# Routing in two parts: three experts' first tiles ahead of the last batch, and the loads of v on another queue

## The chip, the cores and the metric

The kernel runs on one core of one Trainium2 chip. The metric is device microseconds (us) from launch to end. Three runs of the kernel before took 190.79, 191.17 and 836.14 us; the median is 191.17. The program runs its engines from queues of instructions, one for each engine, in the order in which the program lists them: TensorE (PE in the profile), VectorE (DVE), ScalarE (ACT), GpSimd (POOL) and SyncE (SP). SyncE, ScalarE and GpSimd also issue transfers (DMAs), which run on 16 shared transfer engines.

## The reference

```python
scores = q @ k^T / 8                      # 4 batches, 8 heads, 768 positions, 64 per head, float32
# heads 0, 2, 6: causal; the others: causal and (first 4 positions or the last 64)
attn = softmax(masked scores) @ v
x = attn as 3072 tokens of 512            # token = (batch, position)
do_compute = x @ w_skip > 0
e = argmax(x @ w_gate) ; g = max softmax  # 8 experts
out = x ;  out[do_compute] += g * relu(x @ w1[e]) @ w2[e]      # w1 512 x 1024, w2 1024 x 512, float32
```

## The kernel before, in words

**Two plans.** All work is given to a small planner, class `Plan` (L53). `op(name, eng, dur, fn, deps, key)` lists one step with the engine, an assumed duration, what it needs and a key; `dma(...)` (L71) lists a step that issues a transfer and a second one on a queue "Q", which stands for the transfer engines. `lay` (L77) goes through time: whenever an engine is free, the ready step with the smallest key starts. What comes out is only an order: `write` calls the steps' functions in the order of their planned starts, and each engine's queue holds its instructions in that order. On the chip each instruction waits for what it needs, and everything behind it on its engine waits with it. The first plan holds attention and routing, the second the experts.

**Attention.** 16 pairs of heads, numbered `i`, four to a batch. For a pair, SyncE loads q and k (`load_pair`, L644, issue at L650, 384 KB each, in pieces of 6 x 64 floats) into 12 shared buffers, so a load waits for the cast (`Cq`, `Ck`, L702) six pairs before. v comes for a whole batch (`load_v`, L654, issue at L661, pieces of 64 floats): batch 0's in two parts, batches 1 to 3 in one, all on SyncE, into two buffers `vf`. GpSimd casts q, k and v to float16 (L702, `Cv` L708) and lays out parts of k and v for the windowed heads (`Kx` L777, `Vx` L813). TensorE transposes (L730, L741), computes scores (`E`, L876 and L888), ScalarE takes the exp (`X`, L898), TensorE weighs v (`PV`, L940), which also carries the products of v with `w_gate` and `w_skip` as 9 more columns (L795). VectorE divides (`Nr`, `Nl`, `Nx`, L959 to L976); after each batch SyncE stores x to `out` (`xo`, L985; the last batch in three parts) and VectorE sums the batch's logits (`Gs`, L991).

**Weights.** `w1` and `w2` of 8 experts are 16 tiles of 1 MB in float16 (`w1_0` is tile 0, `w2_0` tile 1, ...). GpSimd issues them (L439), cast on the way, mostly in halves of 512 KB. Six tiles have room of their own during attention; `PARTS` says after which step each half may be issued, and in which order:

```python
PARTS = [("Vx", i) for i in (9, 9, 10, 10, 13, 14, 14, 15)]
PARTS += [("r", 0, "R", 12), ("r", 0, "L", 15), ("r", 0, "L", 15)]
```

The other tiles take room that attention leaves, in the second plan.

**Routing** (`route`, L1051). Each token that computes gets a slot: expert `e` has 256 slots, two tiles of 128, `t = 2e` and `2e + 1`. Tokens are 24 columns of 128; columns 0 to 17 are the first three batches, 18 to 23 the last. Phase 0 handles 18 columns, phase 1 the last 6: maximum, expert, one-hot (L1106 to L1115), on TensorE the ranks within the expert (L1088 to L1095), two tables (L1156, L1164 and L1172), and on TensorE the product of the tables, which puts token number and gate into the slots (`slots`, L1193). In the kernel before, both phases add up in one product and one index, `idx` and `gsl` (L1246 to L1250): no tile is known until phase 1 is done. Phase 0's tables are made on GpSimd, phase 1's on VectorE.

**Experts.** For each tile ScalarE writes zeros (`z`, L1281), GpSimd gathers the rows of `out` by `idx` (L1286), VectorE casts (`cx`, L1313), TensorE transposes (`tx`, L1322), VectorE copies (`ox`, L1333). For an expert, first product on both tiles at once (`F`, L1344, 256 columns), ReLU on ScalarE (`Re`, L1354), second product for each tile (`Y`, L1365), VectorE scales and adds (`A`, L1371), GpSimd scatters the rows back (`S`, L1299). One list, `gorder`, fixes the order of gathers and of the remaining halves of weights on GpSimd (a half, two gathers, a half, ...), with at most eight of them on their way. The last tile, 15, comes in a half and two quarters.

## Time and profile before

| what | us |
|---|---|
| median of three runs | 191.17 |
| the profiled execution, its own time | 192.18 |
| its span, first to last instruction | 190.5 |
| busy: PE, DVE, ACT, POOL | 148.3, 108.6, 102.3, 133.0 |
| `idx` written (start of L1248) | 107.88 |
| first gather, first product of an expert | 108.95, 115.33 |
| last weights waited for | 180.32 |

The page divides the span into 40 slices of 4.76 us; each digit is a busy share in tenths, and 9 is 90% or more. The DMA row is the mean share of the 16 transfer engines. In a table by stage, each line has the stretch, its length, busy time and count for PE, PEld (weight load of TensorE), DVE, ACT and POOL, then the clock that TensorE was granted, the share of the transfer engines, and GB/s. Packets of two queues can overlap on one engine, so a share can be a little over 1. A line of the timeline has the start, the length, the engine, the line of the kernel, the operation and its operands; what stands in brackets is the idle time before it and what ended it. "SPq" is SyncE's queue: an issue that lasts long stands at the head of the queue and holds what is behind it.

### The profile page before, as it was taken

How to read it: one execution, taken by the hardware profiler on the slowest of the kernel's cores; microseconds unless marked ns; L12 is line 12 of the kernel's file. 1: busy time of each engine (PE TensorE's matmuls, PEld its weight loads, DVE VectorE, ACT ScalarE, POOL GpSimd, SP SyncE). 2: the span in 40 equal slices, each digit the busy share in tenths (PEclk: the TensorE clock that was granted, in tenths of full speed). 3: DMA queues.
4: the chain of work that ended last, by engine and by line, in shares of the span. 5: the costliest groups of instructions: out<-in, count | busy, mean ns of one | idle time of the engine just before them, and what ended most of it. 6: DMA issues, size and time to landing. Idle time of an engine off the chain costs nothing.

```text
span 190.5 us, 4641 instructions
## 1 busy us (share of the span) xinstructions
PE 148.3 (78%) x1832; PEld 117.2 (62%) x1832; DVE 108.6 (57%) x234; ACT 102.3 (54%) x137; POOL 133.0 (70%) x233
## 2 busy tenths in 40 slices
PE   0688988399999999999922118799999999999700
PEld 0567776388988888878722007768687695638300
DVE  6576457436788769798999524356556434032020
ACT  2595977268899898999769700440340430402100
POOL 7575985969999999987599188788885234354540
PEclk9999999889999999999996555999999999999975
DMA  5999959997899699999999978999999999999720
GB/s 169 332 342 317 313 159 357 385 363 249 242 373 376 193 333 268 213 284 284 213 247 272 206 131 221 227 261 246 223 229 212 191 242 214 243 236 245 189 91 3
DMA packets 29184, 47.12 MB, mean 247 GB/s; under 512 B 5204, under 2 KB 21460, under 8 KB 29154
## 3 DMA queue, kind: packets, MB, share of 16 engines
q0 software_dynamic: 7312, 21.55, 53.1%
q1 hardware_dynamic: 20512, 24.78, 39.4%
q10 hardware_dynamic: 1330, 0.41, 0.9%
q8 instruction: 16, 0.26, 0.6%
q14 instruction: 14, 0.11, 0.2%
HBM read 56.64 MB, written 10.49 MB: 352 GB/s over the span
## 4 chain that ended last, share of the span: by engine, by line
DMA 33%; PE 25%; SPq 11%; DVE 10%; POOL 9%; issue 7%; ACT 2%; POOLq 0%; ACTq 0%
DMA w<-in_moe_w_dram 18%; SPq L650 10%; PE pst L888 8%; DMA out_dram<-xg,idx 6%; PE pst L876 6%; PE opsa L940 4%; POOL xg L1286 3%; DMA kf<-in_k_dram 3%; PE tps L730 3%; DMA xg<-out_dram,idx 3%; POOL out_dram L1299 3%; DMA qf<-in_q_dram 2%; PE tps L741 2%; DVE k L770 2%; ACT k L768 1%
## 5 line engine op out<-in xcount | busy, mean ns | idle before, releaser
L898 ACT ACTIVATE at<-pst 128x1024 f16<-128x1024 f32 (+1 forms) x60 | 58.8, 1013 | 12.8 <-PE pst L888 12.4
L1354 ACT ACTIVATE ht<-hps 128x512 f16<-128x512 f32 x32 | 16.7, 602 | 52.2 <-PE hps L1344 46.4
L888 PE MATMUL pst<-qT,k 128*128 128x128 f16 (+2 forms) x308 | 36.0, 236 | 0.1
L1344 PE MATMUL hps<-xT,w 128*128 128x256 f16 x256 | 31.6, 281 | 1.7 <-DMA w<-in_moe_w_dram 1.1
L770 DVE COPY k<-tps 64x768 f16<-64x768 f16 x27 | 25.8, 954 | 11.7 <-PE tps L730 10.3
L1344 PEld LDWEIGHTS <-w 128*128 128x128 f16 x256 | 29.1, 145 | 4.6 <-DMA w<-in_moe_w_dram 2.4
L1365 PE MATMUL yps<-w,ht 128*128 128x512 f16 x128 | 29.6, 379 | 1.3 <-ACTq L1470 1.1
L888 PEld LDWEIGHTS <-k 128*128 128x128 f16 x308 | 24.6, 99 | 9.3 <-issue 2.6
L1299 POOL DMA_INDIRECT out_dram<-xg,idx x16 | 16.6, 1040 | 17.6 <-DMA out_dram<-xg,idx 6.2
L1371 DVE SCALAR_TENSOR_TENSOR xg<-yps,gsl,xg 128x512 f32<-128x512 f32 x16 | 11.8, 749 | 21.5 <-PE yps L1365 20.9
L439 POOL DMA_DIRECT2D w<-in_moe_w_dram x33 | 19.0, 579 | 6.5 <-DMA w<-in_moe_w_dram 6.3
L1286 POOL DMA_INDIRECT xg<-out_dram,idx x16 | 17.3, 1084 | 8.8 <-DVE gsl L1250 4.2
L876 PE MATMUL pst<-smask,identb 128*128 128x512 bf16 (+2 forms) x64 | 22.0, 353 | 1.6 <-ACT at L898 1.6
L940 PE MATMUL opsa<-va,at 128*128 128x74 f16 x392 | 20.7, 199 | 0.6 <-DVE x L976 0.6
L1365 PEld LDWEIGHTS <-ht 128*128 128x128 f16 x128 | 12.2, 98 | 14.7 <-ACTq L1470 1.3
L940 PEld LDWEIGHTS <-at 128*128 128x128 f16 x472 | 19.0, 99 | 0.8 <-DVE x L976 0.8
L1313 DVE CAST x<-xg 128x512 f16<-128x512 f32 x16 | 9.5, 624 | 12.3 <-DMA xg<-out_dram,idx 10.6
L708 POOL CAST va<-vf 128x768 f16<-128x768 f32 x16 | 13.2, 825 | 2.7 <-PE opsa L940 1.6
L976 DVE TENSOR_TENSOR x<-opsa,recs 128x768 f32<-128x768 f32 x15 | 14.2, 943 | 0.0
L702 POOL CAST k<-kf 128x768 f16<-128x768 f32 x15 | 12.3, 822 | 2.3 <-DMA kf<-in_k_dram 1.9
L756 ACT COPY qT<-tps 128x768 f16<-128x768 f16 x16 | 12.8, 798 | 1.9 <-PE tps L730 1.7
L702 POOL CAST q<-qf 128x768 f16<-128x768 f32 x14 | 11.5, 822 | 3.0 <-DMA qf<-in_q_dram 2.3
(131 smaller groups left out, 227.5 us busy)
## 6 DMA issues: line engine op xcount, KB each, us to landing
w<-in_moe_w_dram POOLq DMA_DIRECT2D x31, 512.0 KB
qf<-in_q_dram SPq DMA_DIRECT2D x16, 384.0 KB, 7.4
kf<-in_k_dram SPq DMA_DIRECT2D x15, 384.0 KB, 6.6
out_dram<-x SPq DMA_DIRECT2D x3, 1536.0 KB, 12.5
out_dram<-x SPq DMA_DIRECT2D x1, 768.0 KB, 13.2
out_dram<-x SPq DMA_DIRECT2D x2, 384.0 KB, 10.9
w<-in_moe_w_dram POOLq DMA_DIRECT2D x2, 256.0 KB
kf<-in_k_dram ACTq DMA_DIRECT2D x1, 384.0 KB, 4.4
```

What stands on the lines that cost most here:

```text
L439: nc.gpsimd.dma_start(out=wts[e, half][:, c], in_=(w1r, w2r)[half][e][:, c])
L650: eng.dma_start(out=t.rearrange("p (h n) d -> p h (n d)", n=NQB), in_=rows6[w][i // 4, :, h0:h0 + 2])
L702: e.tensor_copy(t, f)
L770: nc.vector.tensor_copy(to, ti)
L876: nc.tensor.matmul(pst[:, c0 - c * CH:c0 - c * CH + m].rearrange("p (n c) -> p n c", c=P), identb, mv, start=(n == 0), stop=(n == last))
L888: nc.tensor.matmul(pst[:, c0 - c * CH:c0 - c * CH + m * P], lt, qTs[i][:, qb * P:(qb + m) * P], start=(n == 0), stop=(n == last))
L898: nc.scalar.activation(ats[i][:, c * CH:c * CH + cn], psts[i, c][:, :cn], ACT.Exp, scale=SCALE)
L940: nc.tensor.matmul(opss[i][:, hi, qb * VA:(qb + 1) * VA], ats[i][:, b0 + c:b0 + c + P], vb, start=(n == 0), stop=(n == len(todo) - 1))
L1286: h = nc.gpsimd.indirect_dma_start(out=xgs[:, t], out_offset=None, in_=out[:, :], in_offset=bass.IndirectOffsetOnAxis(ap=idx[:, t:t + 1], ...
L1299: h = nc.gpsimd.indirect_dma_start(out=out[:, :], out_offset=bass.IndirectOffsetOnAxis(ap=idx[:, t:t + 1], axis=0), in_=xgs[:, t], in_offs ...
L1344: nc.tensor.matmul(hpss[e, f2][:, fi, :], w1[:, s, 2 * f2 + fi], xTs[e][:, s, :], start=(fi == 0 and s == 0), stop=(fi == 1 and s == DS - 1))
L1365: nc.tensor.matmul(ypss[t], hts[e][:, j, s2 * P:(s2 + 1) * P], w2[:, j], start=(j == 0), stop=(j == FS - 1))
```

## The change

1. `load_v` issues batches 1, 2 and 3 on ScalarE's queue, each after a given exp (pairs 0, 4, 8); batch 0 stays on SyncE. 
2. Phase 0 gets an index of its own (`idxA`). The first tile of each expert is filled from the first three batches alone: `full` is the expert's count over them, but at least 128, and phase 1's ranks begin there, so that the last batch's tokens go into the second tile. Where three batches give fewer than 128, the rest of the first tile stays empty. Second tiles are completed by phase 1, whose tables now have 8 columns in place of 16.
3. The first tiles of experts 0, 1 and 2 (`KA = 3`) are gathered after `idxA`, in buffers that attention leaves, and go through cast, transposes, both products, ReLU and add in the first plan, beside phase 1. The second plan has 13 tiles left; first tiles of experts 3 to 7 may also be gathered before `idx`. The scatters of the early tiles come after `idx`.
4. `PARTS` has 12 halves in place of 11, ten of them tied to pairs 8 to 14. `gorder` has a new order. Batch 2's x is stored in two parts.
5. The planner's transfers take turns between queues, several durations are changed, and most keys (`K`) have new values, which may change the order on every engine.

```diff
-    PARTS = [("Vx", i) for i in (9, 9, 10, 10, 13, 14, 14, 15)]
-    PARTS += [("r", 0, "R", 12), ("r", 0, "L", 15), ("r", 0, "L", 15)]
+    PARTS = [("Vx", i) for i in (8, 8, 8, 9, 10, 12, 12, 13, 13, 14)]
+    PARTS += [(("G", 0), "go"), (("G", 4), "go")]
...
-                nc.sync.dma_start(out=vs32[b][:, h0 * NQB:h1 * NQB],
-                                  in_=rows1["v"][b, :, h0 * NQB:h1 * NQB])
+                eng = nc.scalar if b else nc.sync
+                eng.dma_start(out=vs32[b][:, h0 * NQB:h1 * NQB],
+                              in_=rows1["v"][b, :, h0 * NQB:h1 * NQB])
...
+        VAT = (0, 1, 5, 9)
...
-                dma(("ld",) + o, "SP", 0.45, 196.6 * (h1 - h0), load_v(b, h0, h1),
-                    [("Cv", 4 * b - 5)], next(sp),
-                    rate=228 if h1 - h0 == 2 else 305)
+                dma(("ld",) + o, "ACT" if b else "SP", 0.6, 196.6 * (h1 - h0),
+                    load_v(b, h0, h1),
+                    [("Cv", 4 * b - 5), VAT[b] and ("X", VAT[b] - 1, 0)],
+                    -99 if b else next(sp), rate=228 if h1 - h0 == 2 else 300, turn=0.22)
...
-        for b in range(B - 1):
+        for b in range(B - 2):
             dma(("xo", b), "SP", 0.5, 1573, x_out(b, 0, DM),
-                [("Nx", 4 * b + 3)], next(sp) - 2.5 * (b < 2))
+                [("Nx", 4 * b + 3)], next(sp) - 2.5)
+        dma(("xo", 2, 9), "SP", 0.5, 787, x_out(2, 0, 256), [("Nx", 9)], next(sp))
+        dma(("xo", 2), "SP", 0.5, 787, x_out(2, 256, DM), [("Nx", 11)], next(sp))
...
                 if ph:
                     nc.tensor.matmul(
                         rk, ones16,
-                        cnt[:, 0:1, :E].to_broadcast([P, n, E]),
+                        full.unsqueeze(1).to_broadcast([P, n, E]),
                         start=False, stop=True)
+                else:
+                    nc.tensor.matmul(r[:, n * E:(n + 1) * E], ones16,
+                                     cnt[:, 0, :E], start=False, stop=True)
...
+            def rsel_full():
+                v.tensor_mul(rsel, rk(), o)
+                if ph == 0:
+                    v.tensor_scalar(full, T[ph, "rk"][:, n * E:(n + 1) * E],
+                                    float(P), 1.0 / P, ALU.max, ALU.mult)
+                    v.tensor_copy(cnt[:, 0, :E], full)
...
+        def fin_a():
+            m = sm_pool.tile([P, NT, 4], FP32, name="msb")
+            v = nc.vector
+            v.tensor_copy(m, T["mps", 0])
+            for n, (i, g) in enumerate(((idx[:, ::2], gsl[:, ::2]),
+                                        (idx0, gsl0))):
+                v.scalar_tensor_tensor(i, m[:, n::2, 1], float(P), m[:, n::2, 0],
+                                       ALU.mult, ALU.add)
+                v.tensor_tensor(g, m[:, n::2, 2], m[:, n::2, 3], op=ALU.add)
+
+        op("idxA", "DVE", 0.8, fin_a, [("r", 0, "slots")], K["sl"])
...
+        for j in range(0, 2 * KA, 2):
+            op(("zA", j), "ACT", 0.95, zero_a(j), [("Cv", 15)], 146 + j)
+        for a in range(KA):
+            t = 2 * a
+            dma(("G", t), "POOL", 1.05, 150, gather(t),
+                [("zA", t), "idxA", ("xo", 2), ("xo", 2, 9), ("G", t - 2, "go")], 152)
+            op(("cx", t), "DVE", 0.6, cast_a(t), [("G", t), ("tx", t - 4)],
+               165 + a)
+            op(("tx", t), "PE", 0.25, turn_a(t), [("cx", t)], 165 + a,
+               take=("tps", ("ox", t)))
+            op(("ox", t), "DVE", 0.42, out_a(t), [("tx", t), ("Fa", t - 4, 1)],
+               165 + a)
+            for h in range(2):
+                op(("Fa", t, h), "PE", 0.92, first_a(t, h),
+                   [("ox", t), ("W", t, 0), ("W", t, 4), ("X", *seq[-2]),
+                    ("X", *seq[-1]), ("Re", t - 4, 1)], 168 + a)
+                op(("Re", t, h), "ACT", 0.6, relu_a(t, h),
+                   [("Fa", t, h), ("PV", 15, 1), ("Ya", t - 4)], 168 + a)
+            op(("Ya", t), "PE", 1.75, second_a(t),
+               [("Re", t, 0), ("Re", t, 1), ("W", t + 1, 0), ("W", t + 1, 4),
+                ("Nx", 15), ("Nl", 15)]
+               + ([("A", t - 4), ("A", t - 2)] if a % 2 == 0 else []), 168 + a)
+            op(("A", t), "DVE", 0.75, add(t), [("Ya", t)], 168 + a)
...
-        gorder = [("g", 0), ("g", 1)]
-        gets, late = list(range(2, NT)), late
-        while gets:
-            gorder.append(late.pop(0))
-            gorder += [("g", t) for t in gets[:2]]
-            gets = gets[2:]
+        gorder, gets = [], [6, 8, -1, 1, -1, 3, 5, -1, 10, 7, -1, 12, 9, -1, 14, 11,
+                            -1, 13, -1, 15]
+        for t in [-1] + gets:
+            gorder.append(("g", t) if t >= 0 else late.pop(0))
         gorder += late
...
+        for a in range(KA):
+            dma(("S", 2 * a), "POOL", 1.0, 150, scatter(2 * a), ["idxB"], 2 * a)
```

In the diff, `("G", t)` is a gather, its `"go"` the issue; `-1` in `gets` is the next half of weights; `zero_a`, `cast_a`, `turn_a`, `out_a`, `first_a`, `relu_a` and `second_a` do for one tile what the experts' steps above do, the first product on 128 columns.

More of the change, by code (lines that the diff above doesn't have):

```diff
@@ L39 @@
 NT = E * CAP // P
+KA = 3
+N0 = 3 * S
 NPR = B * H // 2
@@ L53 @@
 class Plan:
-    LAT = dict(PE=0.26, DVE=0.1, ACT=0.12, POOL=0.12, SP=0.1, Q=1.9)
+    LAT = dict(PE=0.26, DVE=0.1, ACT=0.12, POOL=0.12, SP=0.1, Q=2.1)
     def __init__(self):
@@ L714 @@
         CASTER["q", 0], CASTER["k", 0], CASTER["q", 1] = "DVE", "ACT", "DVE"
-        took = dict(POOL=0.85, DVE=0.6, ACT=0.85)
+        took = dict(POOL=0.83, DVE=0.6, ACT=0.85)
         for i in range(NPR):
@@ new lines, with zero_a, go, row @@
+        op("idx", "DVE", 0.7, fin, [("r", 1, "slots")], 200)
+        xga = {}
+        def zero_a(j):
+            def go():
+                if j == 0:
+                    xga[0] = v_pool.tile([P, 2 * KA, DM], FP32, tag="v",
+                                         name="xga")
+                nc.scalar.copy(
+                    xga[0][:, j:j + 2],
+                    zero1.unsqueeze(2).to_broadcast([P, 2, DM]))
+            return go
+        def row(t):
+            return xga[0][:, t] if t < 2 * KA else xgs[:, t - 2 * KA]
@@ new lines, in moved, with gather, go @@
+        def moved(h):
+            tc.declare_no_dep(
+                h.ins, group="rows",
+                reason="each token is in one slot, so slots share no row")
+            tc.add_to_no_dep_group("rows", h.ins)
+        def gather(t):
+            def go():
+                n = N if t % 2 else N0
+                moved(nc.gpsimd.indirect_dma_start(
+                    out=row(t), out_offset=None, in_=out[:n, :],
+                    in_offset=bass.IndirectOffsetOnAxis(
+                        ap=idx[:, t:t + 1], axis=0),
+                    bounds_check=n - 1, oob_is_err=False))
+            return go
@@ new lines, in scatter, with go, add @@
+        def scatter(t):
+            def go():
+                n = N if t % 2 else N0
+                moved(nc.gpsimd.indirect_dma_start(
+                    out=out[:n, :], out_offset=bass.IndirectOffsetOnAxis(
+                        ap=idx[:, t:t + 1], axis=0),
+                    in_=row(t), in_offset=None,
+                    bounds_check=n - 1, oob_is_err=False))
+            return go
+        def add(t):
+            return lambda: nc.vector.scalar_tensor_tensor(
+                row(t), ypss[t], gsl[:, t:t + 1], row(t), ALU.mult, ALU.add)
```

310 lines of the change are left out of this document (192 added, 118 removed).

## The prediction

> **What bounds the kernel now.** I read the page first (the slices, the chain, the queues), then a table by stage, then the transfer issues of SyncE, and last the routing and the tail in the timeline.
>
> ```profile
> DMA  5999959997899699999999978999999999999720
> DMA 33%; PE 25%; SPq 11%; DVE 10%; POOL 9%; issue 7%; ACT 2%; POOLq 0%; ACTq 0%
> ```
> The 16 transfer engines stand at 9 nearly everywhere, and transfers and SyncE's issues together lead the chain. So I cut the table by stage at the places where that row dips (the last two columns are the transfer engines' share and GB/s):
> ```profile
> 0.00:3.00 3.00, 0.00 (x0) 0.00 (x0) 1.70 (x5) 0.00 (x0) 2.17 (x11) 1.00 0.22 53
> 3.00:23.00 20.00, 15.04 (x199) 12.07 (x200) 13.04 (x36) 14.86 (x17) 13.84 (x26) 1.00 1.07 336
> 23.00:29.00 6.00, 5.40 (x98) 4.56 (x94) 3.31 (x7) 4.70 (x6) 5.20 (x11) 1.00 0.62 171
> 29.00:44.00 15.00, 11.29 (x171) 9.72 (x172) 7.59 (x14) 8.84 (x11) 10.89 (x20) 0.89 1.06 364
> 44.00:48.00 4.00, 3.81 (x62) 3.15 (x60) 2.87 (x6) 3.49 (x5) 3.65 (x9) 1.00 0.70 226
> 48.00:53.00 5.00, 5.00 (x93) 4.42 (x91) 4.37 (x8) 4.51 (x6) 4.77 (x12) 1.00 0.90 259
> 53.00:63.00 10.00, 10.00 (x181) 8.77 (x179) 8.39 (x16) 9.34 (x11) 9.16 (x25) 1.00 1.06 375
> 63.00:67.00 4.00, 3.60 (x63) 3.02 (x60) 2.71 (x7) 3.32 (x5) 3.76 (x9) 1.00 0.55 153
> 67.00:110.00 43.00, 30.90 (x540) 26.44 (x538) 35.52 (x82) 36.57 (x51) 34.00 (x64) 0.90 1.06 258
> 110.00:118.00 8.00, 3.80 (x21) 2.94 (x22) 2.29 (x5) 0.00 (x0) 6.47 (x8) 0.50 0.79 175
> 118.00:178.00 60.00, 56.35 (x419) 41.03 (x418) 25.36 (x52) 16.67 (x32) 35.29 (x44) 1.00 1.05 230
> 178.00:190.50 12.50, 3.09 (x14) 1.07 (x12) 1.41 (x2) 0.00 (x0) 3.83 (x4) 0.71 0.23 72
> ```
> Full stages show a share of 1.05 to 1.07. From 3 to 178 us the engines are full but for five holes: 23-29 (6 x 0.38 = 2.28 us), 44-48 (4 x 0.30 = 1.20), 48-53 (5 x 0.10 = 0.50), 63-67 (4 x 0.45 = 1.80) and 110-118 (8 x 0.21 = 1.68), **7.46 us** in all. That the share is a real limit, and not a queue that is merely never empty, shows in a stretch that holds weights alone and in one that holds them with the scatters:
> ```profile
> 74.00:82.00 8.00, 8.00 (x137) 6.85 (x136) 6.67 (x14) 7.17 (x9) 7.58 (x15) 1.00 1.05 205
> 126.00:160.00 34.00, 33.80 (x254) 24.31 (x252) 17.55 (x39) 9.47 (x19) 20.99 (x26) 1.00 1.05 224
> w<-in_moe_w_dram POOLq DMA_DIRECT2D x31, 512.0 KB
> ```
> A half of a weight tile, 512 KB as it lands, takes 0.524/0.205 = 2.56 us by the first row, 32 halves 82 us. After 126 us the rate hardly moves. TensorE is full there too, but it isn't what ends last: at the end it waits for weights.
> ```profile
> 180.32 1.02 PE L1365 MATMUL yps<-w,ht 128*128 128x512 f16 x4 [0.26 <-DMA w<-in_moe_w_dram]
> 180.95 1.41 DVE L1371 SCALAR_TENSOR_TENSOR xg<-yps,gsl,xg 128x512 f32<-128x512 f32 x2 [5.70 <-PE yps L1365]
> ```
> The last weights land at 180.3; from there 10.2 us of product, add, scatter and close remain, and the change leaves that tail alone. So I forecast when the transfers are done: what the transfers weigh, plus their holes.
>
> **Where the holes are from.** The issues of SyncE (start, length):
> ```profile
> 13.63 0.71 SPq L661 DMA_DIRECT2D vf<-in_v_dram  x1
> 14.39 10.14 SPq L650 DMA_DIRECT2D qf<-in_q_dram  x1
> 34.31 0.71 SPq L661 DMA_DIRECT2D vf<-in_v_dram  x1
> 35.17 8.92 SPq L650 DMA_DIRECT2D qf<-in_q_dram  x1
> 51.09 0.71 SPq L661 DMA_DIRECT2D vf<-in_v_dram  x1
> 51.89 13.77 SPq L650 DMA_DIRECT2D qf<-in_q_dram  x1
> ```
> Each load of v for a batch is issued in 0.71 us, and then the next load of q stands in the queue for 8.9 to 13.8 us: until 24.5, 44.1 and 65.7. The three larger early holes lie at exactly these ends. So SyncE is let go only when the engines have nearly run dry, and they stay thin until new loads flow. Four holes, 5.78 us, I put down to this.
>
> **The change part by part.**
>
> *v of batches 1 to 3 on ScalarE's queue.* Nothing stands behind v on SyncE then, and q and k of later pairs are issued while v moves. Gain: between 0 (the hole goes elsewhere) and 5.78 us. I take three quarters, **4.3 us**, nearer the upper end because the stalls and the holes coincide three times out of three; not all, because a pair's load still waits for the cast six pairs before it, and once these buffers are full the engines may thin out again. The hole at 63-67 is covered twice: ten halves of weights are now tied to the pairs up to 14, from pair 8 on, where eight were tied to 9 to 15. The cost on ScalarE is three issues at 0.71 us by the rows above. Queued behind each is an exp, which the weighing on TensorE awaits; 2.1 us at most if nothing covered them. Attention has room to pay:
> ```profile
> 20.00:38.00 18.00, 13.46 (x212) 11.40 (x211) 10.42 (x17) 12.38 (x15) 14.70 (x29) 0.96 0.91 300
> 38.00:95.00 57.00, 55.93 (x950) 48.15 (x948) 44.05 (x91) 50.05 (x56) 48.83 (x110) 0.98 0.98 283
> ```
> TensorE idles 4.5 us from 20 to 38, where the first stall of SyncE over 10 us is felt, and 1.1 us in the 57 after it. With q and k ahead of v, attention ends some 3 us earlier, which by itself is worth nothing at the end: it brings the buffers free sooner. I count the three issues at 0.
>
> *The split routing.* The tables of the first three batches are made on GpSimd after the last pair as before; what is new is a slot product and five small VectorE operations, then three gathers.
> ```profile
> 98.90 4.76 POOL L1164 TENSOR_TENSOR tables<-r_ohi,r_olo 128x384 f16<-128x384 f16 x6
> 103.24 1.15 PE L1193 MATMUL mps<-tables 128*128 128x64 f16 x18
> 107.88 0.19 DVE L1248 SCALAR_TENSOR_TENSOR idx<-msb 128x16 int32<-128x16 f32 x1
> 108.95 1.09 POOL L1286 DMA_INDIRECT xg<-out_dram,idx  x1 [4.21 <-DVE gsl L1250]
> 113.68 1.13 PE L1322 MATMUL xtp<-ident,x 128*128 128x128 f16 x8 [6.09 <-DVE x L1313]
> ```
> The tables end at 103.7. Product and index take 1.15 + 5 x 0.19 = 2.1 us, less the 3 us that attention may gain: first early gather near 103 to 106 in place of 108.95, first early transposes 4.7 us behind it (108.95 to 113.68), near 108 to 111. SyncE's part is one more issue for batch 2's x, early enough to be landed. GpSimd's queue to idx is now: gather, half a tile, two gathers, two halves, two gathers (experts 3 and 4), a half, and then the gather that waits for idx. These four halves are 4 x 2.56 = 10.2 us of transfers, and cover the hole at 110-118. I take **1.2 us** of its 1.68 (bounds 0 and 1.68), since some descriptors are still written while the engines wait.
> What the wait holds up: behind that gather stand all later weights on GpSimd. VectorE's own path to idx loses two operations of 0.2 us, and may have the casts, copies and adds of three tiles ahead of it:
> ```profile
> L1371 DVE SCALAR_TENSOR_TENSOR xg<-yps,gsl,xg 128x512 f32<-128x512 f32 x16 | 11.8, 749 | 21.5 <-PE yps L1365 20.9
> L1313 DVE CAST x<-xg 128x512 f16<-128x512 f32 x16 | 9.5, 624 | 12.3 <-DMA xg<-out_dram,idx 10.6
> L1333 DVE COPY xT<-xtp 128x512 f16<-128x512 f16 x16 | 6.6, 423 | 10.6 <-PE xtp L1322 10.3
> ```
> 3 x (0.75 + 0.62 + 0.42) = 5.4 us: idx comes between 0.4 us earlier and 5.4 us later, from about 105. Their keys (165 to 168) stand behind the routing's (150), so I take 1 us. The 10.2 us of halves cover all of it; without them it would cost up to 5.4.
>
> *Three tiles multiplied early.* An expert takes 7.39 us of TensorE from one first product to the next:
> ```profile
> 137.93 3.66 PE L1344 MATMUL hps<-xT,w 128*128 128x256 f16 x32
> 145.32 1.47 PE L1344 MATMUL hps<-xT,w 128*128 128x256 f16 x12
> ```
> Half of it for each of three tiles, 11.1 us, moves ahead of idx. 13 tiles are left, 13/16 x 8 x 7.39 = 48 us; even from 120 they end at 168, ahead of the last weights. So this part frees TensorE and moves the end by **0**: weights arrive at 2 x 2 x 2.56 = 10.2 us an expert, and 7.39 us of work hides under that. The zeros on ScalarE, the 16 gathers and the 16 scatters keep their number.
>
> **Sum.** 4.3 + 0 + 1.2 + 0 = 5.5 us off the span of 190.5: 185.0. The profiled execution itself took 192.18 us, so 186.7; the median of the runs is 191.17, so **185.7**.
>
> **Rivals.**
>
> *All holes close, and the end thins out less.* 7.46 us, and about 1.5 us more of the last stretch before 180.3, where TensorE, now ahead, no longer delays scatters: 191.17 - 9.0 = 182.2. For it: v on its own queue and earlier weights cover most holes twice. Against: loads still wait for buffers.
>
> *The queue is not the cause.* Transfers from either queue end on the same 16 engines; if the thinning belongs to v's own end, moving its issue saves only the 0.71 us of issuing, the holes move with v, and 1.2 us is left: 190.0. For it: the engines were over 1.0 while SyncE stood, so nothing was lost then. Against: the next q is issued only when the hole is there.
> The Trainium skill has this as a rule (DMA: Bandwidth & Descriptors, "Issuing engines are not separate DMA queues"): starting transfers from several engines saves only the time to issue them; by that rule this rival is the outcome, and the trace bears it out as far as share and rate go, not for what stands behind v.
>
> *Slower: v starves beside q and k.* Two queues now share the engines. By the loads in the code a piece of q or k is 6 x 64 x 4 = 1,536 bytes and one of v 64 x 4 = 256, and the page has packets of both kinds:
> ```profile
> DMA packets 29184, 47.12 MB, mean 247 GB/s; under 512 B 5204, under 2 KB 21460, under 8 KB 29154
> 24.20 0.82 POOL L708 CAST va<-vf 128x768 f16<-128x768 f32 x1
> ```
> If the queues alternate piece by piece, v has 256/1,792 = 14% of the 336 GB/s; if they share evenly, half. 1.57 MB then takes 33 or 9 us from about 11: batch 1's v lands between 20 and 44. Its first cast stood at 24.2 in GpSimd's queue, with later casts of q and k behind it, for which TensorE waits. It decides once v lands after 33.8: 24.2, the 4.5 us that TensorE now idles, and 2 x 2.56 us of the two halves more that are tied to pairs and keep the engines full. At 39, halfway from there to the end, attention is 5 us late, with batch 2 as late again 10 us, and half of the gains remain: 191.17 + 10 - 2.7 = 198.5. No row shows loads of both kinds from two queues side by side, so I can't exclude it.
> The Trainium skill (DMA: Bandwidth & Descriptors, "Queues, rings and completion order") says that each engine takes turns between its queues by whole packets of several descriptors; by that rule, with several pieces to a packet, v's part is nearer the 14%, and no run here shows it yet.
>
> **How the numbers follow.** Forecast 0.53 (own range 183.5 to 188.0), all holes 0.13, queue not the cause 0.23, slower 0.11. A measurement of this kernel tells about 2% from no change: the bounds are 187.35 and 195.0. Faster: 0.50 of the forecast and 0.13, 0.63; within: 0.03 and 0.23, 0.26; slower 0.11. The range, 182.0 to 191.0, leaves out half of the second case and the slow one, 0.17.
>
> **What would show it.** Right: no issue of q over 5 us behind v; shares near 1.05 from 23 to 67 and from 110 to 118; first products on TensorE before 112, and TensorE waiting for weights from 130 on; the last weights near 175 with 10 us behind them. Wrong: holes of the same size after v has moved; a v cast waiting for its transfer; a gap in the weights while GpSimd waits for idx.

## The result, and the profile after

The changed kernel takes 208.37 us (median of 4 runs, 207.52 to 210.04) against 190.98 for the kernel before beside it: a ratio of 1.0951 with a 95% interval of 1.0835 to 1.1067. It is 17.4 us slower; I had forecast 5.5 us faster. Its profiled execution took 209.07 us, with a span of 207.4. Executions of one kernel scatter (its profiled one and its median can lie 2 to 4 us apart, and one run of the kernel before and one of e8 below took 836 us), so profiles below say where time lies, and medians and ratios how much it is; for two experiments the scatter leaves no ratio.

The row of the transfer engines and the chain on the page of the changed kernel:
```profile
DMA  6999949999949918999999950599999999999310
PE 32%; DMA 25%; issue 14%; POOL 12%; DVE 8%; ACT 6%; ACTq 0%; POOLq 0%
```
Transfers no longer lead the chain. Where the row had shallow dips it now has a 5, a 0 and a 5 in slices 24 to 26, and a 1 in slice 15, counted from 1. The table by stage of the changed kernel, with the cuts of the prediction and some new ones (columns as there; the last two are the transfer engines' share and GB/s):
```profile
23.00:29.00 6.00, 5.24 (x89) 4.34 (x87) 4.71 (x8) 4.35 (x5) 4.21 (x10) 1.00 0.57 170
44.00:48.00 4.00, 4.00 (x62) 3.55 (x61) 1.87 (x4) 3.14 (x5) 1.99 (x6) 0.72 1.05 369
53.00:63.00 10.00, 9.88 (x171) 8.67 (x170) 8.74 (x17) 9.25 (x11) 7.63 (x15) 1.00 0.75 262
63.00:67.00 4.00, 3.93 (x71) 3.45 (x69) 2.95 (x7) 3.38 (x5) 3.53 (x14) 1.00 1.12 347
67.00:80.00 13.00, 10.56 (x176) 8.83 (x174) 7.61 (x15) 10.00 (x12) 12.46 (x25) 1.00 0.64 165
110.00:118.00 8.00, 1.41 (x15) 1.16 (x16) 4.35 (x18) 0.00 (x0) 4.91 (x5) 0.57 1.02 292
118.00:134.00 16.00, 12.98 (x126) 9.77 (x123) 3.71 (x7) 8.07 (x11) 3.64 (x4) 0.90 0.37 73
```
The holes at 44-48, 63-67 and 110-118 are closed, as forecast (though with attention later, as shown below, these times hold other work than before). The one at 23-29 is as it was (0.57, before 0.62). New ones stand at 53-63 (10 x 0.31 = 3.1 us against a full share of 1.06), 67-80 (13 x 0.42 = 5.5) and, above all, 118-134 (16 x 0.69 = **11.0**). In sum 19.6 us of new holes; gone are those at 44-48, 48-53, 63-67 and 110-118 (1.4 + 0.8 + 2.0 + 2.2 = 6.4 by the same measure, less 0.3 left at 110-118). That leaves 13.5 of the 16.9 us between the two spans.

What happens at 118-134, from the timeline and the waits of GpSimd, ScalarE and TensorE in the changed kernel:
```profile
109.13 0.17 DVE L1300 SCALAR_TENSOR_TENSOR idx<-msb 128x8 int32<-128x8 f32 x1
110.19 1.12 POOL L1342 DMA_INDIRECT xga<-out_dram,idx  x1 [2.22 <-DVE r_gate L1164]
114.53 1.18 POOL L460 DMA_DIRECT2D w<-in_moe_w_dram  x2
116.69 0.17 DVE L1312 TENSOR_TENSOR idx<-msc 128x8 int32<-128x8 f32 x1
124.25 3.11 PE L1397 MATMUL hpa<-xTa,w 128*128 128x128 f16 x48
128.43 4.82 ACT L1475 COPY xg<-zero 128x1024 f32<-128x1024 f32 x5
129.75 1.06 POOL L1342 DMA_INDIRECT xg<-out_dram,idx  x1 [14.04 <-ACT xg L1475]
132.15 0.60 POOL L460 DMA_DIRECT2D w<-in_moe_w_dram  x1
```
The three early gathers go out, two halves of weights follow at 114.5, and then GpSimd stands for 14.0 us before the gather of tile 6, the first of the second plan. It waits for ScalarE to write its zeros, and these start only when the last early first product has ended (124.25 + 3.11 = 127.4). The half of weights behind it leaves at 132.15. So from 120 to 132 there is little to move. The index is not what it waits for: tile 6 needs only `idxA` (109.13), and even the full index was there at 116.7.

The reason lies in the storage. The rows of the second plan, `xg`, are 10 tiles in a pool (`moe_xg`) that is opened after the pool of the weights (`moe_w`), and so lies over attention's buffers for q and k in float16. The early tiles keep their cast and transposed rows (`x16a`, `xTa`) in these very buffers (pool `qk`, tags `q16` and `k16`). The zeros may not be written until TensorE has read them for the last time.

Attention ends later too, by 105.72 - 98.23 = 7.5 us, where I had it some 3 us earlier. The last pair's division, in the kernel before and in the changed one:
```profile
98.23 0.22 DVE L959 RECIPROCAL recs<-opsa 128x12 f32<-128x12 f32 x1
```
```profile
105.72 0.23 DVE L987 RECIPROCAL recs<-opsa 128x12 f32<-128x12 f32 x1 [1.34 <-PE opsa L968]
```

### The profile page after: what moved, and what is told of

The parts are those of the page before. It is cut to its first block, busy times and chain, and to the rows that moved or that the text cites. A ratio compares the mean times of both kernels' runs of the same rounds, so it can differ in the third digit from the quotient of the medians.

```text
span 207.4 us, 4844 instructions
## 1 busy us (share of the span) xinstructions
PE 154.8 (75%) x1929; PEld 123.3 (59%) x1929; DVE 108.1 (52%) x241; ACT 102.2 (49%) x140; POOL 132.8 (64%) x233
## 4 chain that ended last, share of the span: by engine, by line
PE 32%; DMA 25%; issue 14%; POOL 12%; DVE 8%; ACT 6%; ACTq 0%; POOLq 0%
PE pst L916 8%; DMA out_dram<-xg,idx 7%; DMA w<-in_moe_w_dram 6%; PE hps L1520 6%; DMA xga<-out_dram,idx 5%; PE opsa L968 5%; DMA qf<-in_q_dram 4%; PE pst L904 4%; PE tps L758 4%; ACT at L926 3%; POOL out_dram L1352 3%; PE yps L1543 2%; DVE k L798 2%; DMA kf<-in_k_dram 2%; POOL q L730 2%
## 5 line engine op out<-in xcount | busy, mean ns | idle before, releaser
L1531 ACT ACTIVATE ht<-hps 128x512 f16<-128x512 f32 x26 | 13.7, 602 | 46.0 <-PE hps L1520 34.2
L1520 PE MATMUL hps<-xT,w 128*128 128x256 f16 (+1 forms) x256 | 28.0, 273 | 3.8 <-DMA w<-in_moe_w_dram 3.8
L1520 PEld LDWEIGHTS <-w 128*128 128x128 f16 x256 | 25.9, 148 | 6.5 <-DMA w<-in_moe_w_dram 5.0
L1543 PE MATMUL yps<-w,ht 128*128 128x512 f16 x104 | 24.2, 382 | 0.0
L1342 POOL DMA_INDIRECT xg<-out_dram,idx x10 | 10.7, 1067 | 16.8 <-ACT xg L1475 14.0
L1360 DVE SCALAR_TENSOR_TENSOR xg<-yps,gsl,xg 128x512 f32<-128x512 f32 x10 | 7.4, 750 | 22.7 <-PE yps L1543 22.3
L1352 POOL DMA_INDIRECT out_dram<-xg,idx x10 | 10.0, 1002 | 13.4 <-DVE xg L1360 7.1
L1543 PEld LDWEIGHTS <-ht 128*128 128x128 f16 x104 | 10.1, 99 | 10.9 <-issue 0.7
L805 POOL COPY kx<-k 64x256 f16<-64x256 f16 x20 | 8.2, 412 | 10.6 <-DVE k L798 6.0
L758 PE MATMUL tps<-ident,k 128*128 128x128 f16 x96 | 8.3, 224 | 6.2 <-ACT k L727 6.2
L784 ACT COPY qT<-tps 128x768 f16<-128x768 f16 x16 | 12.8, 800 | 0.1
```

The source lines that it names most:

```text
L758: nc.tensor.matmul(t[:, n], c16[w, i][:, n].rearrange("p h d -> p (h d)"), C.ident, is_transpose=True, start=(n == 0), stop=(n == NQB - 1))
L1352: moved(nc.gpsimd.indirect_dma_start(out=out[:n, :], out_offset=bass.IndirectOffsetOnAxis(ap=idx[:, t:t + 1], axis=0), in_=row(t), in_offs ...
L1520: nc.tensor.matmul(hpss[e, b][:, fi, :], w1[:, s, m * b + fi], xTs[e][:, s, :w], start=(fi == 0 and s == 0), stop=(fi == m - 1 and s == DS ...
L1543: nc.tensor.matmul(ypss[t], hts[e][:, j, n * P:(n + 1) * P], w2[:, j], start=(j == 0), stop=(j == FS - 1))
```

## The experiments

Theory after the first look: the changed kernel loses most by the room that `xg` shares with the early tiles, and the rest by a later attention. Rivals: the order on ScalarE or the split itself is at fault; v on ScalarE's queue does gain, as forecast, and only the rest costs. All ratios are against the kernel before on the same chip.

### Is it the room? (e1, e2)

```diff
-    with tc.tile_pool(name="moe_w", ...) as mw_pool, \
-         tc.tile_pool(name="moe_xg", ...) as xg_pool, \
+    with tc.tile_pool(name="moe_xg", ...) as xg_pool, \
+         tc.tile_pool(name="moe_w", ...) as mw_pool, \
```


> Changed kernel, with the buffer for the second plan's 10 tiles allocated ahead of the weight tiles, so that it lies over the buffers of the loads of q and k (read for the last time during attention) and no longer over the buffers that the early tiles' cast and transposed rows use. Theory 'storage': gather 6 waited 14 us on GpSimd for early tiles to be done with that room, and all weights stood behind it; the thin stretch of the transfer engines from 120 to 134 (10.4 us) goes, and the time falls from 208.4 to about 198. Rival 'the early tiles themselves are too slow or too late': the transfers stay thin there for another reason, 205 to 208.

Measured: 197.58 us, ratio 1.0448 [1.0373, 1.0523]. Two lines changed places and 10.8 us are gone between the medians, 5.0 points (hundredths) of the ratio. The stretch in this kernel:
```profile
118.00:134.00 16.00, 14.20 (x147) 10.95 (x145) 6.48 (x12) 3.36 (x6) 12.60 (x15) 0.91 1.05 246
```
The share is 1.05 where it was 0.37.

```diff
-            return lambda: nc.scalar.copy(xgs[...], zero1...)
+            return lambda: nc.gpsimd.memset(xgs[...], 0.0)
...
-            op(("z", t), "ACT", 0.95, zero(t, t + 2), key=t - 100)
+            op(("z", t), "POOL", 0.95, zero(t, t + 2), key=-101 - NT + t)
```


> Changed kernel, with the zeros of the second plan's tiles written by GpSimd in place of ScalarE, room unchanged. Theory 'storage': the zeros must still wait for the early tiles' products, so gather 6 comes at 127 to 130 as before and the time stays at 206 to 210. Rival 'queue order': the zeros were late only because they stood behind the early tiles' ReLUs on ScalarE; gather 6 then goes at about 118 and the time falls to about 198.

Measured: 207.39 us, ratio 1.0948 [1.0854, 1.1043], so nothing. The wait of GpSimd in this kernel names what the zeros wait for on any engine:
```profile
POOL xg L1475 <- PE hpa L1397: 10.1, 1, 10.1
```
The early first product (`hpa`) holds the room, and the time is where the theory had it. ScalarE's order is not the cause.

### Does v on ScalarE's queue gain? (e3, e4)

```diff
-                eng = nc.scalar if b else nc.sync
+                eng = nc.sync
```


> Changed kernel, with v of batches 1 to 3 issued on SyncE again, all else as changed (the planner lays out the rest anew). Theory 'v on ScalarE costs': attention ends about 8 us sooner (98 in place of 105.7) and the time falls to 200 to 202. Rival 'the new keys and durations order attention worse': attention stays late and the time is 206 to 209.

Measured: 206.98 us, 1.0917 [1.0818, 1.1017]. The theory missed. The time is in the rival's range, though not for its reason: attention does end 3.9 us sooner (101.78), but the time hardly moves, and the wait for room is 15.2 us in place of 14.0.

v on ScalarE's queue alone, put into the kernel before (the planner lays out the order anew around it):
```diff
-                nc.sync.dma_start(out=vs32[b][...], in_=rows1["v"][b, ...])
+                eng = nc.scalar if b else nc.sync
+                eng.dma_start(out=vs32[b][...], in_=rows1["v"][b, ...])
```


> Kernel before, with nothing changed but v of batches 1 to 3 on ScalarE's queue, at the same steps as in the changed kernel. Theory 'v on ScalarE costs': a later load on SyncE waits for v to land, through one of the eight completion semaphores that both queues share, and ScalarE waits for loads of q and k ahead of v; attention ends 5 to 8 us later, 196 to 199 against 191. Rival 'keys': 189 to 192. My prediction's own term: 4.3 us faster, 186 to 188.

Measured: 197.51 us, 1.0449 [1.037, 1.0528]. The part that I priced at 4.3 us of gain costs 8 us by itself. Rows of its table by stage, and two of SyncE's waits and issues:
```profile
23.00:29.00 6.00, 3.76 (x65) 3.02 (x62) 2.19 (x3) 4.37 (x5) 4.23 (x10) 1.00 1.07 375
53.00:63.00 10.00, 9.99 (x165) 8.62 (x164) 8.04 (x15) 9.14 (x11) 9.42 (x22) 1.00 0.50 167
80.00:95.00 15.00, 14.10 (x254) 12.12 (x251) 12.45 (x28) 12.54 (x15) 10.62 (x25) 1.00 0.80 199
```
```profile
SPq L650 <- DMA vf<-in_v_dram: 5.4, 1, 5.4
```
```profile
51.41 0.37 SPq L650 DMA_DIRECT2D kf<-in_k_dram  x1
```
All holes from 23 to 53 are closed (1.08 at 44-48, 1.06 at 48-53), just as my theory of SyncE's stalls wanted. But the last load of k is issued at 51.4 where the last loads of before were issued at 65.7; from 53 to 63 little is left, because the weights stay tied to later pairs. The holes have moved (5.6 us at 53-63, 3.1 at 67-80, 3.9 at 80-95), and TensorE pays at the start: 3.76 us of work in 23-29 in place of 5.40. Attention ends at 101.32, 3.1 us later than before; I had expected 5 to 8. SyncE also still waits for v: in the program the loads of both queues count in turn on the same eight completion semaphores, so the load whose turn comes back to v's semaphore waits until v has landed (in e4 14.4 us after its issue, at 26.6): 5.4 us here and, in the changed kernel, 12.8:
```profile
SPq L674 <- DMA vf<-in_v_dram: 12.8, 1, 12.8
```

### Both undone; keys (e5, e6, e7)

The room first, and v on SyncE:

> The changed kernel with both suspects undone: room for the gathered rows taken ahead of the weights' (as in the run with the swap), and v of batches 1 to 3 back on SyncE. Theory (two causes that add): the swap alone gave 197.6 against 208.4; v on ScalarE cost about 8 us in the kernel before; so 197.6 - 8 to 197.6 - 4 = 190 to 194, attention's last pair divides near 101.5, the transfer engines' share from 120 to 134 stays near 1.0. Rival (new keys and the new order of weights cost as much by themselves): 195 to 198.

Measured: 194.82 us, 1.0351 [1.0251, 1.045]; between theory and rival. The last pair divides at 103.94, not 101.5. Two waits in its trace looked like what is left; e9 and e12 below take each of them up. In attention, at 70 to 75 us, ScalarE's next exp waits 5.0 us for TensorE's weighing of v, whose cast (issued at 69.97) stood behind casts of later q and k on GpSimd:
```profile
ACT at L926 <- PE opsa L968: 5.0, 1, 5.0
```
And from 110 to 115 there is a hole, since after the half at 95.27 the next weights stand behind the first gathers:
```profile
110.00:115.00 5.00, 0.34 (x6) 0.24 (x6) 2.47 (x13) 0.00 (x0) 3.20 (x3) 0.50 0.18 38
```
```profile
95.27 0.59 POOL L460 DMA_DIRECT2D w<-in_moe_w_dram  x1
111.19 1.49 POOL L1342 DMA_INDIRECT xga<-out_dram,idx  x1 [3.19 <-issue]
114.98 0.61 DVE L1369 CAST x16a<-xga 128x512 f16<-128x512 f32 x1 [1.96 <-DMA xga<-out_dram,idx]
115.30 1.20 POOL L460 DMA_DIRECT2D w<-in_moe_w_dram  x2
```

The same with the old values of the keys `K`:

> The same kernel with the key values of the kernel before, so that attention is in the order it had. Theory (what remains late in attention is the order the keys give): the last pair divides near 98 to 99 and the time is 186 to 190, since the split routing now closes the hole at 110-118 (my 1.2 us). Rival (keys are no cause): as the run without the old keys, within 1 us.

Measured: 201.01 us (199.32 to 205.67, no ratio). Missed by both: the old keys are no good in the new planner. It says nothing on which keys are better.

> The same as the kernel with both suspects undone, but no tile is gathered and multiplied in the first plan (KA = 0); the index is still made in two parts. My step 'early tiles move the end by 0': same time within 1 us as that kernel. Rival (early tiles sit on VectorE and GpSimd in the way of the index): 2 to 4 us faster. Other rival (early tiles do help the end): 2 to 4 us slower.

Measured: 196.91 us, 1.04 [1.0286, 1.0514]. With `KA = 0` alone the list of gathers no longer names tiles 0, 2 and 4, so this kernel doesn't gather the rows of three tiles; its time answers nothing. The question is put again in e10 and e15.

### Are the holes SyncE's stalls? (e8)

In the kernel before, v of batches 1 to 3 in quarters:
```diff
-                 ("v", 0, 2, H), ("q", 2), ("k", 2), ("q", 3), ("k", 3),
-                 ("q", 4), ("k", 4), ("v", 1, 0, H)]
-        for i in range(5, NPR):
-            order += [("q", i), ("k", i)]
-            if i in (7, 11):
-                order.append(("v", (i + 1) // 4, 0, H))
+                 ("v", 0, 2, H), ("q", 2), ("k", 2), ("q", 3), ("k", 3)]
+        for i in range(4, NPR):
+            h = 2 * (i % 4)
+            order += [("q", i), ("k", i), ("v", i // 4, h, h + 2)]
```


> The kernel before with v of batches 1 to 3 in quarters of two heads, one behind the q and k of each pair, all on SyncE. My reading of the holes (SyncE stands behind one big load of v for 9 to 14 us and the engines run dry): the holes at 23-29, 44-48 and 63-67 shrink and the time is 185 to 188. Rival (loads end when buffers let them, the hole only moves; what is missing is weights to fill in): 188.5 to 191, with a new hole later in attention.

Measured: 195.29 us, 1.0277 [1.0124, 1.043]; both were wrong. The holes do close (the share is 1.17 at 23-29, 1.08 at 44-48 and 0.98 at 63-67), and pair 12 divides at 81.2 in place of 84.6. Then, in its trace, VectorE waits:
```profile
DVE x L974 <- DMA out_dram<-x: 6.7, 1, 6.7
DMA to landing us min/median/max: 4.4/11.3/22.6
```
The rows of batch 3 go into the buffer of an earlier batch, and that batch's store took up to 22.6 us to land, where the longest store of the kernel before took 13.2:
```profile
DMA to landing us min/median/max: 8.8/12.5/13.2
```
Moving transfers earlier has closed these holes and made another transfer late; that this one wait is the whole loss is not shown.

### The ties of the weights (e9, e11, e12)

e5 with the last two early halves tied as before:
```diff
-    PARTS += [(("G", 0), "go"), (("G", 4), "go")]
+    PARTS += [("r", 0, "R", 12), ("r", 0, "L", 15)]
```


> The changed kernel with the room swapped and v on SyncE (194.8 us), and the last two early halves of weights tied to the routing tables again, as before the change, in place of the first and third gather. Theory: with them behind the first gather nothing is left for the transfer engines from 107 to 115 (share 0.18 from 110 to 115); given back, the share from 110 to 118 goes from 0.41 to 0.8 or more, some 3 to 4 us are saved, 191 to 192. Rival (what is late is idx and the gathers, whose landing the weights only delay): 194 to 195.5.

Measured: 195.71 us, 1.0246 [1.0113, 1.038]: no gain that can be told, as the rival had it. The hole at 110-118 did close by more than half (share 0.41 to 0.81, 3.2 us), while 118-126 thinned from 1.05 to 0.91. TensorE's waits from 112 us on, in e5 and then here:
```profile
PE xtpa L1377 <- DVE x16a L1369: 4.3, 2, 3.6
PE hps L1520 <- DMA w<-in_moe_w_dram: 1.4, 1, 1.4
```
```profile
PE xtpa L1377 <- DVE x16a L1369: 4.3, 2, 3.5
```
TensorE doesn't wait for a single weight any more. So I took the end to be set by TensorE, from its first tile on, and that tile to be held up by the landing of its rows; e16 tests it.

The kernel before with the new ties for the first ten halves:

> The kernel before with only the ties of the weights changed: ten halves tied to pairs 8 to 14 as in the change, and one to the tables. My step 'the hole at 63-67 is covered by earlier weights': that hole (1.8 us) closes and the time is 187 to 188.5. Rival (the issues stand in front of casts on GpSimd, attention ends later, and the table's two halves are missed at 103-110): 190 to 193.

Measured: 195.39 us (191.61 to 199.86, no ratio; the profile is the run at 199.86, the longest, so its rows may show more than the other three runs had). The rival is nearer. The hole at 63-67 closes. In exchange v of the last batch comes late beside the weights, and SyncE stands for 20.0 us where it stood for 13.8:
```profile
50.93 20.04 SPq L650 DMA_DIRECT2D qf<-in_q_dram  x1
```
```profile
POOL va L708 <- DMA vf<-in_v_dram: 6.8, 1, 6.8
```

e9 with `Cv=-230.5` in place of -204.5:

> As the run with the halves tied to the tables, with one key changed (Cv from -204.5 to -230.5), which sets the casts of v further ahead on GpSimd. Theory (what keeps attention 5.7 us later than before is the order on GpSimd: pair 8 waits 5 us for a v cast that stands behind casts of k and q of later pairs): the last pair divides near 99 to 100 and the time falls by 2 to 4 us, to 188 to 190. Rival (attention's end isn't what sets the time, or the wait only moves to another cast): as that run, within 1 us.

Measured: 195.35 us, 1.0272 [1.0155, 1.039]. Attention ends 2.8 us sooner (101.13) and the time stays, as the rival said. A new hole of 2.3 us comes at 67-80, and the gain is gone before the experts begin: the first gather goes out only 0.5 us sooner than in e9 (111.08 against 111.57), behind two halves of weights issued at 107.31, and its rows are cast 4.8 us later (115.89), so TensorE's first transposes come at 116.56, later than e9's 115.73.

### Early products (e10)

```diff
-KA = 3
+KA = 0
...
-        gorder, gets = [], [6, 8, -1, 1, ...
+        gorder, gets = [], [0, 2, 4, 6, 8, -1, 1, ...
```


> As the run with the halves tied to the tables, but without early products: the first tiles of experts 0 to 2 are gathered first of all in the second plan, all 16 tiles are multiplied there. My step 'three tiles multiplied early move the end by 0': within 1 us of that run. Rival (they do shorten the end): 2 to 4 us slower. Other rival (they stand in the way of idx on VectorE): 2 to 3 us faster.

Measured: 198.49 us, 1.0467 [1.0362, 1.0573], 2.8 us slower than e9 on the same chip (all four runs took 198.2 to 199.4, three of e9's four 194.2 to 196.6). The early products do shorten the end. My 0 was wrong, to the good.

### The split alone (e13, e14, e15)

Attention wholly as before: old planner, durations, keys, ties and stores, v on SyncE. The order on SyncE is the same instruction for instruction, on the others up to about pair 13. Of the change, e13 keeps the split routing and the early tiles, with the rows' room ahead of the weights'. e14 is e13 with the room where the change has it; e15 is e13 with no early tiles, all 16 in the second plan; the half of weights that e13 ties to the first early gather is tied to the last table (`("r", 0, "L", 15)`) there, since that gather is gone.
```diff
+    PARTS = [("Vx", i) for i in (9, 9, 10, 10, 13, 14, 14, 15)]
+    PARTS += [("r", 0, "R", 12), ("r", 0, "L", 15), ("r", 0, "L", 15)]
+    PARTS += [(("G", 0), "go")]
```


> Only the second and third parts of the change (split routing, three early tiles), with the rows' room ahead of the weights' room; attention wholly as before: its planner, durations, keys, ties of the weights, stores, v on SyncE. Theory (the rest of the loss, 195 against 190, is attention's new order, which ends 4 to 6 us later): the last pair divides near 98.2 and the time is 188 to 191, no slower than before. Rival (the split itself costs, through its operations on VectorE and three more gathers in the first plan): 193 to 196.

> The same kernel with the rows' room where the change has it, behind the weights', over the buffers of the early tiles. Theory (the gather of tile 6 and all weights behind it wait for the early products): POOL waits 12 to 15 us for zeros, the time is 9 to 12 us over the run with the room ahead. Rival (with attention's old order the early tiles are done in time and nothing waits): within 2 us of it.

> As the run with attention as before and the room ahead, but all 16 tiles in the second plan (KA = 0). On the changed attention the early products were worth 2.8 us. Theory (TensorE, from its first tile on, is as near the end as the weights are, so moving 11 us of its work ahead of idx is worth 2 to 3 us): 2 to 3 us slower. Rival (my step, 0): same within 1 us.

Measured: e13 192.01 us, 1.0136 [1.0064, 1.0208]; e14 203.41, 1.075 [1.0673, 1.0827]; e15 193.87, 1.024 [1.0154, 1.0326]. The room costs 11.4 us on the old attention too. The wait of GpSimd in e14:
```profile
POOL xg L1319 <- ACT xg L1452: 16.5, 1, 16.5
```
The early products gain 1.9 us between the medians; the two intervals overlap, and the moved half is part of that difference, so e10 is the cleaner case. But the split as a whole, mended, is still slower than the kernel before, by 1.4 us between the medians and about 2.6 by the ratio, though in the profile of e13 (a run at 190.0, its fastest) the first gather starts 3 us before that of the kernel before and the hole at 110-118 is closed:
```profile
110.00:118.00 8.00, 4.05 (x37) 3.92 (x38) 2.37 (x4) 0.00 (x0) 6.47 (x8) 0.50 1.05 268
160.00:178.00 18.00, 18.00 (x116) 12.01 (x115) 4.50 (x6) 4.13 (x8) 8.08 (x9) 1.00 0.89 208
```
```profile
102.23 1.12 POOL L443 DMA_DIRECT2D w<-in_moe_w_dram  x2
105.94 1.22 POOL L1319 DMA_INDIRECT xga<-out_dram,idx  x1 [2.60 <-issue]
107.17 0.59 POOL L443 DMA_DIRECT2D w<-in_moe_w_dram  x1
112.73 0.64 DVE L1346 CAST x16a<-xga 128x512 f16<-128x512 f32 x1 [5.22 <-DMA xga<-out_dram,idx]
113.43 0.61 PE L1354 MATMUL xtpa<-ident,x16a 128*128 128x128 f16 x4 [6.84 <-DVE x16a L1346]
```
From 160 to 178 TensorE is full (18.00 of 18) and the transfers thin out (0.89): the bound has changed. And TensorE starts at 113.43, no sooner than before (113.68), because the first rows need 6.8 us from gather to cast (105.94 to 112.73) beside three halves of weights. In e5, where the share was 0.18 at that time, they needed 3.8 (111.19 to 114.98).

e13 shows one thing more. SyncE's instructions are those of the kernel before, and GpSimd's, ScalarE's and VectorE's have the same order until after 70 us. Its stalls are nearly the same (9.2, 9.4 and 12.7 us), and yet its holes are small:
```profile
49.98 12.71 SPq L657 DMA_DIRECT2D qf<-in_q_dram  x1
23.00:29.00 6.00, 5.87 (x106) 5.08 (x103) 4.06 (x8) 5.48 (x8) 5.04 (x11) 1.00 0.84 252
63.00:67.00 4.00, 4.00 (x73) 3.43 (x71) 2.47 (x3) 3.71 (x5) 3.74 (x8) 1.00 0.90 268
```
With 0.92 at 44-48 and 0.99 at 48-53 the four early holes are 1.7 us here (3.2 in e16), by the prediction's own measure, where the one profile of the kernel before had 5.78. And attention ends at 98.4 in e13 and 98.6 in e16, against 98.2. So neither the size of the holes nor the end of attention follows from the stalls; what makes the holes differ between executions stays open.

### Which limit ends last? (e16, e17)

```diff
-    PARTS += [("r", 0, "R", 12), ("r", 0, "L", 15), ("r", 0, "L", 15)]
-    PARTS += [(("G", 0), "go")]
+    PARTS += [("r", 0, "R", 12), ("r", 0, "L", 15)]
+    PARTS += [(("G", 4), "go"), (("G", 4), "go")]
```


> The split on attention as before, with the room ahead (192.0 against 190.6), and two halves of weights moved: one from ahead of the first gather and one from right behind it to behind the third. Theory (TensorE, busy from its first tile to the end, now sets the time, and its first tile waits 6.8 us from gather to cast because three halves share the engines with it; with engines idle it was 3.4 to 4.0): first early cast near 110 in place of 112.7, time 189 to 190.5, about 2 us less. Rival (weights set the end, so a hole of 2 us at 106-110 comes back in full): 192 to 194.

Measured: 189.24 us, ratio 0.998 [0.9941, 1.0019]. The median is 2.8 us under that of e13, and the two intervals of the ratios don't meet; the time is that of the kernel before. (The profiled spans, 188.2 and 187.3, lie only 0.9 apart, since e13's profile is its fastest run.) Its rows:
```profile
106.12 1.20 POOL L1319 DMA_INDIRECT xga<-out_dram,idx  x1 [3.12 <-issue]
109.97 0.61 DVE L1346 CAST x16a<-xga 128x512 f16<-128x512 f32 x1 [2.29 <-DMA xga<-out_dram,idx]
```
The first early cast has come forward by 2.8 us, as expected: it stands 3.9 us behind its gather in place of 6.8. TensorE waits for no weights in this kernel, and from 134 to 160 it is busy without a gap (26.00 of 26).

One more half goes behind the third gather (`("r", 0, "R", 12)` and then three times `("G", 4)`):

> As that run, but no half of weights is issued from the pair before the last routing table to the third gather: three halves stand behind it. Theory of TensorE at the end: first cast near 109.5, but a hole of some 4 to 5 us in the weights, so both limits meet: 189 to 192. Rival (weights set the end): 195 to 197.

Measured: 191.56 us, 1.0108 [1.0058, 1.0159]. The cast comes 0.8 us earlier still (109.15), but the engines now stand half idle, and TensorE waits for weights again:
```profile
103.00:110.00 7.00, 1.18 (x22) 0.92 (x20) 4.25 (x20) 0.00 (x0) 3.67 (x4) 0.50 0.57 154
```
```profile
PE hps L1497 <- DMA w<-in_moe_w_dram: 1.0, 2, 0.5
```
So the two limits lie within about a half of weights (2.56 us) of each other. None of the versions beats the kernel before.

## Why the prediction was wrong, point by point

**The step that failed** is this one: "behind that gather stand all later weights on GpSimd ... The 10.2 us of halves cover all of it". The risk was the right one, and I looked at the wrong gather. I followed the first gather that waits for `idx`, and counted the gathers of tiles 6 and 8 ahead of it as free, since `idxA` was there. I asked for every instruction what data it waits for, not what storage it writes. The whole diff shows `x16a` and `xTa` taken from attention's q and k buffers, and `xg` in a pool over them. Price: 10.8 us (e1), 11.4 on the old attention (e14), between medians. What I had as cover, four halves, was two halves issued at 114.5: 5.1 us, by the prediction's 2.56 each, against a wait of 14.0. The runs show in its place that the first gather of the second plan, with all weights behind it, waits for the early tiles' products through the room.

**v on ScalarE's queue, 4.3 us of gain**: wrong in sign, about +8 us by itself (e4); in the changed kernel 2.8 between the medians (e5 against e1), where the intervals of the ratios overlap. From the hole lying at the end of the stall I concluded that the stall makes the hole. Taking the stalls away does close the holes (e4 and e8), but e13 has the same stalls with less than a third of the holes: I had priced the holes of one execution. And a closed hole was no gain. Loads that go out earlier run out earlier; with the weights tied to pairs the hole comes back behind them (53-63 in e4) or an x store, a v load or a cast comes late (e8, e11, e5). My rival "The queue is not the cause" was nearer with its holes that move, but not with its 190.0. The rival "Slower" has e4's time (198.5 against 197.5), and that is luck: by its reason v had to land after 33.8, and in e4 it landed at 26.6, 14.4 us after its issue. What the Trainium skill says (DMA: Bandwidth & Descriptors, "Issuing engines are not separate DMA queues"), that issuing from another engine saves only the time of issuing, agrees with these runs: e4 moved the same loads and won nothing.

**"The hole at 63-67 is covered twice" by earlier weights**: it closes, and nothing is gained: e11 is slower, and in its trace v and q come later beside the weights.

**The split, 1.2 us**: the hole at 110-118 closes and the first gather comes at 105.94, inside my 103 to 106, when attention isn't late (e13). What I mis-sized is "first early transposes 4.7 us behind it": 7.5 (105.94 to 113.43). I took the 4.7 from a row that lay in the very hole I meant to fill.

**Early tiles, 0**: 1.9 (e15) to 2.8 us (e10) of gain. I put 48 us for 13 tiles under the weights and concluded that TensorE has slack. In e9, e13 and e16 it waits for no weights, and from 134 to 160 it is busy for 25.07, 26.00 and 26.00 us of 26: there the slack is gone.

**The method**, transfers plus holes, explains the loss well (13.5 of 16.9 us in holes) but not the mended kernels: once holes are filled, TensorE from its first tile on is the second limit, within about a half of weights of the first (e16 and e17). That the end of the transfers sets the end of the kernel was true in the one trace I had.

Going back step by step, in points of the ratio to the kernel before on each run's own chip: the room takes 5.0 of the 9.5 points (1.0951 to 1.0448, e1), v's queue 1.0 (to 1.0351, e5; not clear of the scatter), attention's new order with its planner, ties, stores and keys 2.1 (to 1.0136, e13), and the weights issued too near the first gather 1.6 (to 0.998, e16). A point is 1.9 us. That most of what e5 still loses lies in attention's new order was shown only as a whole, by e13. It isn't attention's end alone, which e12 moved for nothing; which ties or keys it is stays open.

## What to carry to other kernels

When work is moved into an earlier phase, list for each buffer that it borrows what the next phase puts into that place, and which in-order queue stands behind the first write to it. A gap on a shared resource that you fill is worth its length only if nothing else was using the gap: look at what landed quickly because of it. When two limits end within a few us of each other, price a change against both.

## What the runs showed of the hardware

The first products after the routing run on a slow TensorE. The granted clock is 0.50 from 110 to 118 in the kernel before, in e13 and in e5. The first 32 early products of e13, and 32 of the same shape 16 us later:
```profile
114.55 3.57 PE L1374 MATMUL hpa<-xTa,w 128*128 128x128 f16 x32 [0.52 <-DVE xTa L1363]
130.44 2.12 PE L1497 MATMUL hps<-xT,w 128*128 128x128 f16 x32 [0.95 <-DVE xT L1482]
```
They take 1.7 times as long, so some of the time that early tiles gain is lost to the clock. In e16 TensorE works nearly without a gap from 112.25 on, and the clock is 0.50 until 117 and 1.00 from 118, 0.51 on the mean of this stretch:
```profile
110.00:118.00 8.00, 6.71 (x62) 6.20 (x63) 2.91 (x6) 1.08 (x2) 6.78 (x8) 0.51 1.01 223
```
The Trainium skill (TensorE: Matmul & The Clock Gate, "Part 1: The HAM clock gate (the "warmup" mystery)") has TensorE at half clock after an idle stretch, and warm again after about 3.4 us of sustained work, counted in a window that runs freely. The half clock agrees with the 0.50; coming back took some 5 to 6 us here, which lies between one and two such windows.
